# Attention with a feature map and an MLP mixer on one core: contracting the plain projections over 128 rows instead of 64

## The chip, the cores and the metric

The kernel runs on one core of one Trainium2 chip, in one launch. The metric is the device time of that core in microseconds, given as the median of three runs. A profiled execution has a time of its own and a span, which is the time from its first to its last instruction.

## The reference

For 8 batches of 8 heads, q, k and v have 576 tokens of 64 numbers. The feature map projects every token of q and k by the same 64 x 128 matrix, takes off the largest absolute value of the row, and joins exp(x) and exp(-x):

```python
def phi(x):
    proj = np.einsum('bhsd,df->bhsf', x, w_phi)
    proj = proj - np.max(np.abs(proj), axis=-1, keepdims=True)
    return np.concatenate([np.exp(proj), np.exp(-proj)], axis=-1)
```

From the mapped keys come kv (256 x 64 for each head) and z, their sum over tokens; the output of a head is phi(q) kv / (phi(q) z + 1e-6). The heads side by side give x, 576 x 512 for each batch. A token mixer follows, u = x + (relu(x^T W1) W2)^T with W1 576 x 256 and W2 256 x 576, and a channel mixer, u + relu(u C1) C2 with C1 512 x 1536 and C2 1536 x 512.

## The kernel before, in words

The 64 heads are worked on as 32 pairs. The first seven pairs (`PLAIN = 7`) are called plain: their attention matmuls are in float32, each of which TensorE runs as two passes. For a plain pair, `load_plain` (line 659) brings tiles named `pair` of 128 rows: rows 0 to 63 hold q, transposed, and rows 64 to 127 hold k. The other pairs take their rows split into a high and a low part (tiles `stk`, `stq`) against `wp2`.

`less_max` (line 611) makes the projection. For a plain pair it gets `base`, 64 for keys and 0 for queries, and contracts the 64 rows from there with the same 64 rows of `wp`, which holds the 64 x 128 matrix twice, one copy under the other. The output of one unit is 128 tokens x 128 features in a PSUM tile, named `ppk` for keys, `ppq` for queries and `ppt` for the odd 64 tokens of both queries of a pair. A plain pair has nine units of keys and nine of queries. VectorE then takes the largest absolute value (`mxk`, `mxq`, `mxt`, line 643) and subtracts it (`pmk`, `pmq`, `pmt`, line 645), and ScalarE makes the exponentials.

After that: `add_kv` (line 758) sums keys times values into `pkv`; `turn` (line 819) transposes the queries (`pt`); `numerators` (line 846) multiplies by kv (`pn`), and the denominators go through memory and back by small DMAs (`row`, `few`, `inv`, `den`). `token_mix` (line 899) has the tiles `px`, `pa`, `ph`; the channel mixer has `up_proj` (`h`) and `down_proj` (`acc`), lines 967 and 982. The mixer's weights come as 64-bit words, which `convert` (line 538) turns into high and low parts by one ScalarE, four VectorE, and again one ScalarE and one GpSimd instruction for each piece (tiles `bits`, `bitsc`).

Nothing is issued while this is written down. Five streams (keys, queries, tokens, weights, channels) record their instructions, and `arrange` (line 274) puts all of them in one order, by costs and due times that it works out itself: a plan of each engine's time, in which `cost` (line 198) gives each instruction a duration. For TensorE it holds a pass on part of the rows apart from a pass on all (lines 436 to 444): a part may run beside a part on other rows, and a change between parts and the whole costs 90 ns (`TURN`). It also keeps an own picture of TensorE's clock from an estimate of the work in it (`op.work`, line 215), in which a pass on 64 rows counts half. The order on TensorE prefers tokens, then keys and queries, then channels (lines 241 to 247). Setting up `wp` and `wp2` has lines 522 to 526; all recorded instructions show line 175 in the profile, so that they are told apart by their tiles.

Of the kernel before, what the change touches and what calls it, by code (L numbers as in the profile page):

```python
# [8 lines left out]
F32 = mybir.dt.float32  # L9
# [8 lines left out]
P = 128  # L18
B, H, S, D = 8, 8, 576, 64
NP = H // 2  # L20
F = 128
# [456 lines left out]
def mixer_kernel(ctx, tc, qk, qkp, vals, w_phi, w1, w1t, w2, wc1, wc2d, out):  # L478
    real, nc = tc.nc, Recorder()

    def pool(name, bufs, kind="sbuf", **kw):
        return Pool(ctx.enter_context(tc.tile_pool(name=name, bufs=bufs, **kw)), kind, bufs)

    cst = pool("cst", 1)
    wk = pool("wk", 2)
# [14 lines left out]
    def split(hi, lo, raw, eng_hi, eng_lo):  # L500

        if eng_hi is nc.scalar:
            nc.scalar.copy(hi, raw)
        else:
            eng_hi.tensor_copy(hi, raw)
        eng_lo.tensor_tensor(lo, raw, hi.bitcast(F32), op=ALU.subtract)
# [13 lines left out]
    eps = odd.tile([P, 1], F32, tag="eps", name="eps", bufs=1)  # L520
    nc.gpsimd.memset(eps, 1e-6)
    wp2 = st.tile([P, 2, F], F32R, tag="wp2", name="wp2", bufs=1)
    wp = cst.tile([P, F], F32, name="wp")
    nc.scalar.dma_start(wp[D:], w_phi)
    nc.scalar.dma_start(wp[:D], w_phi)
    split(wp2[:, 0], wp2[:, 1], wp, nc.vector, nc.vector)

    w1_h = cst.tile([P, 5, T], F32R, name="w1_h")
    w1_l = cst.tile([P, 5, T], F32R, name="w1_l")
# [81 lines left out]
    def less_max(ts, units, name, base=None):  # L611

        n, kind = len(units), name[0]
        if base == D and nplain["k"] < 5 * OPEN:
            ps = ps_a.tile([P, 2, 2, F], F32, tag=f"a{nplain['k'] % 2}", name=f"pp{name}")
        elif base == 0 and (nplain["q"] % 2 == 0 or nplain["q"] >= BORROWED):
            ps = ps_h.tile([P, 2, 2, F], F32, tag="h", name=f"pp{name}")
        elif kind == "k" or base == 0:  # L620
            ps = ps_w.tile([P, 2, 2, F], F32, tag="keys", name=f"pp{name}", bufs=1)
        else:
            ps = ps_w.tile([P, 2, 2, F], F32, name=f"pp{name}", **REST)
        if base is not None:
            nplain["k" if base else "q"] += 1
        for i, u in enumerate(units):
            t, c = (ts[1], 512) if u is None else (ts[u[0]], P * u[1])
            if base is None:
                nc.tensor.matmul(ps[:, i].rearrange("p two f -> p (two f)"), t[:, c:c + P],
                                 wp2.rearrange("p two f -> p (two f)"), start=True, stop=True)  # L630
            else:
                rows = slice(base, base + D)
                nc.tensor.matmul(ps[:, i, 0], t[rows, c:c + P], wp[rows], start=True, stop=True)
        if base is None:
            part = wk.tile([P, 2, F], F32, tag="part", name=f"part{name}")
            nc.scalar.copy(part[:, :n], ps[:, :n, 1])
            pr = wk.tile([P, 2, F], F32, tag="p", name=f"p{name}")
            nc.vector.tensor_tensor(pr[:, :n], ps[:, :n, 0], part[:, :n], op=ALU.add)
            pr, eng = pr[:, :n], nc.gpsimd
        else:  # L640
            pr, eng = ps[:, :n, 0], nc.vector
        mx = odd.tile([P, 2], F32, tag=f"mx{kind}", name=f"mx{name}")
        nc.vector.tensor_reduce(mx[:, :n], pr, axis=AX.X, op=ALU.max, apply_absolute_value=True)
        pm = wk.tile([P, 2, F], F32, tag=f"pm{kind}", name=f"pm{name}", bufs=1 if kind == "t" else 2)
        eng.tensor_tensor(pm[:, :n], pr, mx[:, :n].unsqueeze(2).to_broadcast([P, n, F]), op=ALU.subtract)
        return pm

# [20 lines left out]
    def keys():  # L668
# [3 lines left out]
        for i in range(B * NP):  # L672
# [9 lines left out]
            for g, us in enumerate(groups if i < PLAIN else blocks):  # L682
                pm = less_max(ts, us, f"k{i}_{g}", plain)
                if plain is None and g == 4:
                    kp = wk.tile([P, 1, 2, F], F32, tag="kt", name=f"kp{i}_{g}", bufs=1)
                elif plain is None and g % 2:
                    kp = wk.tile([P, 512], F32, tag="bits", name=f"kp{i}_{g}", bufs=3)
                    kp = kp.rearrange("p (n two f) -> p n two f", n=2, two=2)
                else:
                    kp = wk.tile([P, 2, 2, F], F32, tag="kp", name=f"kp{i}_{g}")  # L690
                for sg in range(2):
                    nc.scalar.activation(kp[:, :len(us), sg], pm[:, :len(us)], AF.Exp, scale=1.0 - 2.0 * sg)
                if plain is None:
                    sums(i, g, kp)
                yield 0.22
                for do, *args in todo:
                    do(*args)
                    yield 0.82
                if plain is not None:
                    todo = [(add_kv, i, g, us, kp, v_sb)]  # L700
                else:
                    todo = [(turn_kv, i, v_sb)] if g == 4 else []
# [82 lines left out]
    def queries():  # L785
# [3 lines left out]
        for piece in pieces:  # L789
            if split_up:  # L790
                yield from until(lambda: split_up[0] in kvs)
                numerators(*split_up)
                yield 0.75
            split_up = None
            if turned:
                split_up = turn(*turned)
                yield 0.25
            turned, made = made, None
            if piece:
                i, k, j = piece  # L800
                if (k, j) == (sides(i)[0], 0):
                    plain = 0 if i < PLAIN else None
                    if i < PLAIN:
                        yield from until(lambda: i in pairs)
                        ts = pairs[i]
                    else:
                        yield from until(lambda: i + 1 in raws or i + 1 == B * NP)
                        if i + 1 == B * NP:
                            load(i + 1)
                        ts = stack(raws[i + 1], 0, f"q{i}")  # L810
                    asked.add(i)
                if (k, j) == (0, 0):
                    tail = less_max(ts, [None], f"t{i}", plain)
                    yield 0.11
                pm = less_max(ts, [(j, 2 * k), (j, 2 * k + 1)], f"q{i}_{k}{j}", plain)
                made = (i, k, j, pm, tail)
                yield 0.22
# [312 lines left out]
```

## Time and profile before

| what | value |
|---|---|
| median of three runs | 1141.4 us (1139.65 to 1142.62) |
| profiled execution, its own time | 1142.8 us |
| span of that execution | 1141.0 us |
| PE busy | 1108.2 us, 97% of the span |
| PEld busy | 1033.7 us, 91% |
| DVE busy | 702.1 us, 62% |
| ACT busy | 629.2 us, 55% |
| POOL busy | 534.5 us, 47% |
| mean granted TensorE clock | 0.996 |

PE is TensorE's matmul stream, PEld its loads of stationary operands, which run beside it; DVE is VectorE, ACT ScalarE, POOL GpSimd, SP SyncE, which issues most DMAs. One pass is one load and one matmul. The ends of matmuls are modelled, so that the distance between the starts of two loads tells more of the pace than the busy time does.

### The profile page before, as it was taken

Reading aid. Unit: us, or ns where it says so; the run is one execution under the profiler, and the core shown is the slowest. Engines: PE = TensorE matmul, PEld = TensorE weight load, DVE = VectorE, ACT = ScalarE, POOL = GpSimd, SP = SyncE. Lnnn points to the kernel's source line nnn. Section 1 sums busy time; section 2 is a strip of 40 time slices with the busy share of each in tenths; the row PEclk is TensorE's granted clock in tenths of the full one; section 3 lists DMA queues with packets and bytes.
Section 4 is the critical chain, followed back from the end, with each engine's and each line's share of the span. In section 5 each row is a group of like instructions: output and inputs, shape, how many; then the busy total and the mean of one; then the engine's idle time right before and its main releaser. Section 6 shows DMA issues by size and latency. Waiting matters only on the chain.

```text
span 1141.0 us, 24085 instructions
## 1 busy us (share of the span) xinstructions
PE 1108.2 (97%) x8862; PEld 1033.7 (91%) x8862; DVE 702.1 (62%) x1558; ACT 629.2 (55%) x1749; POOL 534.5 (47%) x673
## 2 busy tenths in 40 slices
PE   8999999999999999999999999999999999999998
PEld 6788888788899989989999999999999999999998
DVE  4888875786667656767666666767676565211111
ACT  3887655666656566656666665665665555211110
POOL 1233426566556656456566556574664554011110
PEclk9999999998999999999999999999999999999999
DMA  6654521121121211211112111212121111000000
GB/s 180 170 155 133 138 83 46 50 61 40 44 51 45 63 44 45 59 45 48 39 48 59 39 52 44 63 45 58 49 59 24 46 28 31 12 20 20 20 20 20
DMA packets 60166, 65.42 MB, mean 57 GB/s; under 512 B 27344, under 2 KB 47056, under 8 KB 60048
## 3 DMA queue, kind: packets, MB, share of 16 engines
q1 hardware_dynamic: 59744, 63.48, 20.4%
q8 instruction: 70, 1.15, 0.4%
q14 instruction: 48, 0.39, 0.2%
q10 hardware_dynamic: 304, 0.40, 0.1%
HBM read 54.12 MB, written 9.73 MB: 56 GB/s over the span
## 4 chain that ended last, share of the span: by engine, by line
PE 80%; DMA 8%; DVE 5%; POOL 2%; ACT 2%; issue 2%; SPq 0%; ACTq 0%; DVEq 0%; POOLq 0%
PE acc L175 22%; PE h L175 22%; PE pkv L175 8%; PE pn L175 8%; PE pa L175 4%; PE ph L175 4%; PE ppk L175 4%; DMA den<-inv 4%; PE ppq L175 3%; PE pt L175 2%; DMA inv<-few 2%; PE px L175 2%; DMA few<-row 1%; DVE ks L175 1%; PE pkt L175 1%
## 5 line engine op out<-in xcount | busy, mean ns | idle before, releaser
L175 PE MATMUL acc<-gh,wc 128*128 128x256 f32 x1728 | 329.2, 280 | 1.1 <-ACT gh L175 0.9
L175 PEld LDWEIGHTS acc<-gh,wc 128*128 128x128 f32 x1728 | 272.5, 188 | 3.0 <-ACT gh L175 1.9
L175 PE MATMUL h<-uh,wc_h 128*128 128x256 f32 x864 | 242.9, 281 | 0.3 <-DVE gl L175 0.2
L175 PE MATMUL h<-uh,wc_l 128*128 128x256 f32 x864 | 242.3, 280 | 0.0
L175 PE MATMUL h<-ul,wc_h 128*128 128x256 f32 x864 | 242.0, 280 | 0.0
L175 PE MATMUL acc<-gl,wc 128*128 128x256 f32 x864 | 241.3, 280 | 0.0
L175 DVE SCALAR_TENSOR_TENSOR gl<-h,gh 128x512 fp32r<-128x512 f32 x108 | 74.5, 690 | 147.8 <-ACT gh L175 146.9
L175 PEld LDWEIGHTS h<-uh,wc_h 128*128 128x128 f32 x864 | 162.8, 188 | 2.8 <-issue 1.5
L175 PEld LDWEIGHTS h<-uh,wc_l 128*128 128x128 f32 x864 | 162.8, 188 | 0.8 <-issue 0.8
L175 PEld LDWEIGHTS acc<-gl,wc 128*128 128x128 f32 x864 | 162.6, 188 | 0.9 <-issue 0.8
L175 PEld LDWEIGHTS h<-ul,wc_h 128*128 128x128 f32 x864 | 162.6, 188 | 0.8 <-issue 0.8
L175 ACT ACTIVATE gh<-h 128x512 fp32r<-128x512 f32 x108 | 64.7, 599 | 138.0 <-PE h L175 137.3
L175 ACT ACTIVATE kp<-pmk 128x256 f32<-128x256 f32 (+1 forms) x320 | 107.7, 390 | 33.4 <-DVE pmk L175 12.7
L175 POOL TENSOR_TENSOR ql<-qf,qh 128x320 fp32r<-128x320 f32 (+1 forms) x100 | 83.8, 838 | 68.9 <-ACT qh L175 61.3
L175 POOL TENSOR_TENSOR ul<-xt,uh 128x64 fp32r<-128x64 f32 (+3 forms) x120 | 60.4, 533 | 113.9 <-ACT uh L175 113.1
L175 ACT COPY xt<-pn 64x256 f32<-64x256 f32 (+2 forms) x160 | 53.2, 345 | 108.3 <-DVE den L175 72.5
L175 ACT ACTIVATE qf<-pt 128x256 f32<-128x256 f32 (+1 forms) x256 | 103.3, 412 | 15.9 <-PE pt L175 14.3
L175 POOL TENSOR_TENSOR pmk<-pk,mxk 128x256 f32<-128x256 f32 (+1 forms) x125 | 79.7, 642 | 52.0 <-DVE mxk L175 33.0
L175 PE MATMUL pn<-qh,kv 128*128 128x320 f32 (+1 forms) x400 | 99.2, 300 | 2.9 <-DVE pt L175 1.4
L175 POOL TENSOR_TENSOR xt<-xt,den 128x256 f32<-128x256 f32 (+1 forms) x64 | 52.7, 823 | 93.4 <-DMA den<-inv 89.8
L175 POOL TENSOR_TENSOR pmq<-pq,mxq 128x256 f32<-128x256 f32 x100 | 63.6, 638 | 61.4 <-DVE mxq L175 49.7
L175 POOL TENSOR_TENSOR stq<-raw,stq 64x512 fp32r<-64x512 f32 (+1 forms) x50 | 74.1, 1481 | 36.3 <-ACT stq L175 32.5
(111 smaller groups left out, 2455.8 us busy)
## 6 DMA issues: line engine op xcount, KB each, us to landing
raw<-in_qk SPq DMA_DIRECT2D x24, 576.0 KB
rawc<-in_wc SPq DMA_DIRECT2D x24, 512.0 KB
v<-in_vals SPq DMA_DIRECT2D x31, 325.0 KB
den<-inv SPq DMA_DIRECT2D x64, 80.0 KB
den<-inv SPq DMA_DIRECT2D x64, 64.0 KB
out_x<-xt SPq DMA_DIRECT2D x12, 256.0 KB
out_x<-xt SPq DMA_DIRECT2D x16, 192.0 KB
pair<-in_qkp SPq DMA_DIRECT2D x7, 320.0 KB
```

The source lines that it names most:

```text
L175: return getattr(getattr(nc, self.unit), self.name)(*[real(a) for a in self.args], **{k: real(v) for k, v in self.kw.items()})
```

## The change

`wp` becomes two tables beside each other, each 128 rows high: table 0 has the matrix in rows 0 to 63 and zeros below, table 1 has zeros in rows 0 to 63 and the matrix below. A plain projection contracts all 128 rows of its `pair` tile with the table of its side. The split into `wp2` is made in two halves of 64 rows, and the tile `pmt` loses a half that was not used.

```diff
     wp2 = st.tile([P, 2, F], F32R, tag="wp2", name="wp2", bufs=1)
-    wp = cst.tile([P, F], F32, name="wp")
-    nc.scalar.dma_start(wp[D:], w_phi)
-    nc.scalar.dma_start(wp[:D], w_phi)
-    split(wp2[:, 0], wp2[:, 1], wp, nc.vector, nc.vector)
+    wp = cst.tile([P, 2, F], F32, name="wp")
+    for j in (1, 0):
+        rows = slice(j * D, j * D + D)
+        nc.gpsimd.memset(wp[rows, 1 - j], 0.0)
+        nc.scalar.dma_start(wp[rows, j], w_phi)
+    for j in range(2):
+        rows = slice(j * D, j * D + D)
+        split(wp2[rows, 0], wp2[rows, 1], wp[rows, j], nc.vector, nc.vector)
...
             else:
-                rows = slice(base, base + D)
-                nc.tensor.matmul(ps[:, i, 0], t[rows, c:c + P], wp[rows], start=True, stop=True)
+                nc.tensor.matmul(ps[:, i, 0], t[:, c:c + P], wp[:, base // D], start=True, stop=True)
...
-        pm = wk.tile([P, 2, F], F32, tag=f"pm{kind}", name=f"pm{name}", bufs=1 if kind == "t" else 2)
+        pm = wk.tile([P, 1 if kind == "t" else 2, F], F32, tag=f"pm{kind}", name=f"pm{name}",
+                     bufs=1 if kind == "t" else 2)
```

## Rows read from the trace of the kernel before

**Rows 1.** Busy time by stretch: us, PE, PEld, DVE, ACT, POOL, clock, DMA, GB/s.
```profile
9.00:28.40 19.40, 19.40 (x78) 16.39 (x78) 11.85 (x31) 8.38 (x23) 3.04 (x2) 1.00 0.59 157
28.40:60.00 31.60, 29.25 (x209) 24.67 (x208) 27.20 (x74) 27.02 (x76) 7.26 (x8) 1.00 0.56 158
60.00:116.00 56.00, 55.66 (x361) 46.05 (x359) 47.78 (x110) 42.98 (x114) 18.84 (x17) 1.00 0.58 147
116.00:185.00 69.00, 65.58 (x485) 59.19 (x485) 52.30 (x95) 40.62 (x95) 29.63 (x30) 1.00 0.31 93
...
240.00:285.00 45.00, 40.58 (x283) 34.97 (x283) 32.07 (x75) 28.27 (x83) 26.01 (x33) 0.89 0.17 47
285.00:965.00 680.00, 667.82 (x5532) 631.50 (x5531) 453.31 (x1025) 414.44 (x1189) 395.20 (x503) 1.00 0.18 47
965.00:1141.00 176.00, 171.51 (x1500) 171.07 (x1498) 35.20 (x65) 29.56 (x71) 17.34 (x30) 1.00 0.07 20
...
80.00:100.00 20.00, 19.88 (x130) 16.72 (x129) 17.82 (x41) 15.26 (x40) 8.36 (x8) 1.00 0.41 105
```

**Rows 2.** The plain projections' loads, by tile: count, duration ns min/median/max, first and last start.
```profile
L175 PEld LDWEIGHTS ppk<-wp,pair x126: 182/188/335, 3.7 to 116.1; 64*128 64x128 f32 x126
L175 PEld LDWEIGHTS ppq<-wp,pair x112: 182/188/334, 6.4 to 183.0; 64*128 64x128 f32 x112
L175 PEld LDWEIGHTS ppt<-wp,pair x14: 183/186/330, 7.2 to 156.5; 64*128 64x128 f32 x14
```

**Rows 3.** Timeline of PEld, 90 us: start, duration, merged instructions.
```profile
90.17 0.24 PEld L175 LDWEIGHTS pt<-ident,pmq 128*128 128x128 f32 x2
90.58 0.52 PEld L175 LDWEIGHTS ppq<-wp,pair 64*128 64x128 f32 x4 [0.17 <-PE ph L175]
91.22 0.74 PEld L175 LDWEIGHTS pkv<-v,kp 128*128 128x128 f32 x6
```

**Rows 4.** Timeline of PEld, 9 to 13 us.
```profile
9.03 1.78 PEld L175 LDWEIGHTS pkv<-v,kp 128*128 128x128 f32 x8 [0.22 <-issue]
10.99 1.78 PEld L175 LDWEIGHTS ppq<-wp,pair 64*128 64x128 f32 x8 [0.18 <-issue]
13.00 0.29 PEld L175 LDWEIGHTS pt<-ident,pmq 128*128 128x128 f32 x2 [0.22 <-issue]
```

**Rows 5.** Timeline of PEld: runs of 64-row loads, the first, one on the way, the last.
```profile
30.25 0.29 PEld L175 LDWEIGHTS ppt<-wp,pair 64*128 64x128 f32 x2
...
115.98 0.29 PEld L175 LDWEIGHTS ppk<-wp,pair 64*128 64x128 f32 x2
...
182.67 0.52 PEld L175 LDWEIGHTS ppq<-wp,pair 64*128 64x128 f32 x4 [0.43 <-DVE gl L175]
```

**Rows 6.** Timeline of PE: keys and queries side by side, the first, and three at full pace.
```profile
6.36 0.58 PE L175 MATMUL ppq<-wp,pair 64*128 64x128 f32 x1 [1.40 <-DMA wp<-in_w_phi]
...
35.51 0.27 PE L175 MATMUL ppq<-wp,pair 64*128 64x128 f32 x1
35.52 0.27 PE L175 MATMUL ppk<-wp,pair 64*128 64x128 f32 x1
35.62 0.27 PE L175 MATMUL ppq<-wp,pair 64*128 64x128 f32 x1
```

**Rows 7.** Timeline of PE, 24 to 31 us.
```profile
24.62 1.06 PE L175 MATMUL ppk<-wp,pair 64*128 64x128 f32 x4
25.61 2.50 PE L175 MATMUL pn<-qf,kv 128*128 128x320 f32 x4
...
28.40 1.93 PE L175 MATMUL pkv<-v,kp 128*128 128x104 f32 x16
```

**Rows 8.** Timeline of DVE, from 6 us.
```profile
6.42 0.23 DVE L175 CAST wp<-wp 128x128 fp32r<-128x128 f32 x1 [6.42 <-DMA wp<-in_w_phi]
6.68 0.29 DVE L175 TENSOR_TENSOR wp<-wp,wp 128x128 fp32r<-128x128 f32 x1
```

## The prediction

> **What bounds the kernel now.** I read the table of engines first and then the busy time by stretch, because the share over the whole span hides three different stages. After 285 us PE is busy 667.82 of 680 us, and the last 176 us hold almost nothing but the mixer's matmuls, with VectorE at 35.20 [rows 1]. That last stretch is work which TensorE couldn't place earlier. So TensorE's time saved anywhere comes off the end, as long as the instant at which it was saved has something else for TensorE to do. The plain projections all lie before 185 us [rows 2], and there VectorE is near its limit too: 27.20 of 31.6 us, 47.78 of 56, and at its densest 17.82 of 20, a share of 0.89 [rows 1]. Before 28.4 us it has room, 11.85 of 19.4, and PE is busy without a gap.
>
> Busy time hides what matters here, so I then went through the timeline of PEld. There are 126 + 112 + 14 = 252 passes on 64 rows [rows 2], in runs between passes on 128 rows. At 90 us the four loads of such a run last 0.52 us, the last one 0.19, so loads start every (0.52 - 0.19)/3 = 0.11 us. Two loads of pt at 90.17 should let the run begin at 90.39; it begins at 90.58, 0.19 late. Its four loads should let pkv begin at 91.02; it begins at 91.22, 0.20 late [rows 3]. Going to 64 rows and back costs **0.39 us a run**, though PE counts as busy. Transposes, pkv and pn follow each other without such a gap.
>
> Early passes are slower. Between 9 and 13 us eight loads last 1.78 us, (1.78 - 0.33)/7 = 0.21 us each, and the two turns of that run cost 1.96 - 8 x 0.21 = 0.28 and 2.01 - 8 x 0.21 = 0.33 [rows 2, 4]. At 28.40 us sixteen passes of pkv take 1.93 us; eight had taken 1.78 us in loads alone at 9.03 [rows 4, 7]. [...] Up to 24.62 us runs of 64-row passes come between the others all the time; the first stretch without any, pn from 25.61 on, is the one behind which the pace doubles [rows 7].
>
> **The change part by part.** *Turns removed.* The timeline has 39 runs of 64-row passes between 30.25 and 182.67 us: 9 up to 60, 23 up to the one at 115.98, 7 behind it [rows 5]. At 0.39 us that is 3.5, 9.0 and 2.7 us. Between 9 and 28.4 us there are five, at 0.6 us: 3.0 us.
>
> *Overlap lost.* Where a key run and a query run meet, they share the array: at 35.51 and 35.52 one pass of each starts, the next at 35.62, so two passes go in the time of one [rows 6]. I count 32 such pairs from 6.36 us on: 8 at the slow pace, 18 up to 60, 6 later. Contracted over all rows they follow one another: 8 x 0.21 = 1.7, 18 x 0.11 = 2.0, 6 x 0.11 = 0.7 us lost. [...]
>
> *One pass itself.* A 128-row float32 pass with a 128-wide operand isn't in this part of the trace; the nearest, pkv with 104 columns, runs at 0.11 us as the projections do [rows 3, 7], and I take no difference.
>
> *The clock.* The rows bound this by nothing (the pace rises at 28.4 as before) and by a rise as soon as TensorE is filled from 9 us on. I take the second end, nearer to the only rise there is: it came 2.8 us after pn had followed the last 64-row run [rows 7], and the changed kernel has none. With some us for a later start I put it at 13 us. Of the 15.4 us up to 28.4, 2.4 are turns counted above; 13.0 us of slow passes become 6.5.
>
> *What of this VectorE lets through.* In each stretch I take the smaller of TensorE's saving and the time that VectorE would have left at its densest share, 0.89 [rows 1]. From 9 to 28.4: TensorE 3.0 - 1.7 + 6.5 = 7.8, VectorE 19.4 - 11.85/0.89 = 6.1; so 6.1. Up to 60: 3.5 - 2.0 = 1.5 against 31.6 - 27.20/0.89 = 1.0; so 1.0. Up to 116: 9.0 - 0.7 = 8.3 against 56 - 47.78/0.89 = 2.3; so 2.3. Up to 185: 2.7 against 69 - 52.30/0.89 = 10.2; so 2.7. What isn't let through turns into waits of PE for VectorE. The sum is **12.1 us**. If the weights' conversion, which is the movable part of VectorE's work, is put elsewhere by the new order, up to 1.3 + 1.5 + 8.3 + 2.7 + 6.5 = 20.3 us.
>
> *The rest.* Two memsets go to POOL, which is busy 3.04 of 19.4 us just after; they run while the DMAs of the matrix land and cost nothing. The split on VectorE takes four instructions for two, 0.23 + 0.29 = 0.52 us more if half the rows take as long [rows 8], and the first reduction queues behind it; the key half, which lands first, may also leave earlier. I take 0, with ends of -2.7 (the first projections start at 3.7, and the split holds VectorE's queue until 6.42 [rows 2, 8]) and +0.5. `pmt` costs nothing: the same elements are written. The two DMAs stay on ACT's queue in their order. The `pair` and weight loads on SP and the denominators' round trips move with the buffers that they wait for; I find no one queued behind them that isn't also freed sooner. The whole order is worked out anew, since durations and clock in the plan change. That has no row; the nearest is the disturbed stretch from 240 to 285 us, where PE is busy for 40.58 of 45 us and the clock is 0.89: (1 - 0.89) x 45 = 5.0 us [rows 1]. One such stretch may go or come; I take none and keep 5 us either way.
>
> The profiled execution took 1142.8 us: 1142.8 - 12.1 = 1130.7. It stood 1.4 us above the median, so I forecast **1129 us** for the median.
>
> **The rivals.** *All of it arrives.* The new order shifts conversions and VectorE doesn't bind: 1142.8 - 20.3 - 1.4 = 1121 us. For it: VectorE is busy only 52.30 of 69 us behind 116. Against: the weights must be there before the channel mixer can fill TensorE's time.
>
> *The clock rises when it did.* Then the first stretch gives 1.3 and the sum is 7.3: 1134 us. For it: one rise is a thin base, and the rows can't part the missing 64-row runs from other differences. [...]
>
> *Nothing arrives.* VectorE and the denominators' round trips set the pace up to 185 us, and PE's saved time becomes waits: 1141 us. For it: VectorE's 85% between 28 and 116. Against: PE waits there for hardly anything, 55.66 of 56 us busy. That the edit doesn't do what it says would show the same: no run of passes closing up.
>
> *Slower: TensorE outruns VectorE and the clock falls.* Place: 28 to 285 us. Gaps on PE like those between 240 and 285 us take the clock down, and each such stretch costs 5.0 us. Two more of them (10.0) against the low saving of 7.3 leave +2.7, no change; the third decides, 15.0 - 7.3 = +7.7: 1149 us. For it: 6 us of TensorE's saving between 60 and 116 can't pass VectorE. Against: between 28 and 60 VectorE's share is as high, PE has 2.35 us of gaps, and the clock column stays at 1.00 [rows 1].
>
> **How the numbers follow.** The forecast has 0.50, all of it 0.12, the clock unmoved 0.15, nothing 0.13, slower 0.10. A difference of 0.3% (3.4 us) is about what a measurement of this kernel can tell from none. So faster 0.77, within it 0.13, slower 0.10. The range goes from 1119, below the second case, to 1141, which takes in the forecast with 5 us either way, the unmoved clock and part of the fourth; the slower case and some of the ends stay out.
>
> **What would show it.** The loads of ppk, ppq and ppt in the form 128*128, 252 of them, 0.11 us apart with no 0.2 us before and behind. The pace of pkv near 0.11 us from about 13 us on; at 28 us, as before, my clock step is wrong. The run of ppk that stands at 115.98 some 9 us earlier. New waits of PE for mxk, pmk or qf between 30 and 116 us are what VectorE kept back; if they sum to 10 us, nothing arrives. Behind 285 us the passes should be the same and shifted by the gain; a loss there, or a clock under 1.00 in more places than 240 to 285, makes the prediction wrong.

## The result and the profile after

The changed kernel takes **1126.0 us** (median of 4 runs, 1125.26 to 1126.45); the kernel before, run again beside it, takes 1140.6 us. The ratio is 0.987, with a 95% interval of 0.985 to 0.989: 14.6 us faster, where 12.1 were forecast. The profiled execution has a span of 1124.1 us and a time of 1126.0 us. That of the kernel before stood 2.2 us above the new median, so spans alone overstate the gain (16.9 us), and so do the distances that are read from the two traces below.

The busy time by stretch of the changed kernel, with the columns of [rows 1]:

```profile
9.00:28.40 19.40, 18.78 (x143) 17.69 (x142) 16.47 (x45) 13.10 (x36) 1.27 (x1) 1.00 0.47 139
28.40:60.00 31.60, 28.38 (x203) 24.92 (x201) 24.64 (x67) 24.90 (x73) 6.66 (x8) 1.00 0.63 164
60.00:116.00 56.00, 52.66 (x383) 47.28 (x384) 46.06 (x105) 45.86 (x122) 19.11 (x18) 1.00 0.52 147
116.00:185.00 69.00, 59.48 (x451) 54.35 (x451) 61.36 (x106) 39.92 (x89) 38.68 (x36) 1.00 0.33 101
...
240.00:285.00 45.00, 43.38 (x355) 40.85 (x354) 33.19 (x75) 29.13 (x82) 28.60 (x36) 1.00 0.25 64
285.00:965.00 680.00, 672.14 (x5569) 636.60 (x5568) 447.19 (x1021) 414.07 (x1189) 395.36 (x501) 1.00 0.18 46
```

Three things differ from [rows 1]. Between 9 and 28.4 us TensorE gets through 142 loads instead of 78, and VectorE does 16.47 us of work instead of 11.85. Between 28.4 and 185 us PE has more gaps: 3.2 + 3.3 + 9.5 = 16.1 us against 6.1 us before; behind 116 VectorE is at 61.36 of 69, a share of 0.89. And from 240 to 285 us the clock stays at 1.00 (before: 0.89), with 1.6 us of gaps on PE instead of 4.4.

The loads of the keys' projections by tile (as [rows 2]) and the timeline of PEld (as [rows 3, 4]):

```profile
L175 PEld LDWEIGHTS ppk<-wp,pair x126: 186/192/338, 6.3 to 111.0; 128*128 128x128 f32 x126
```

```profile
6.33 1.78 PEld L175 LDWEIGHTS ppk<-wp,pair 128*128 128x128 f32 x8 [6.33 <-issue]
...
10.41 2.45 PEld L175 LDWEIGHTS pkv<-v,kp 128*128 128x128 f32 x14
12.79 0.75 PEld L175 LDWEIGHTS ppq<-wp,pair 128*128 128x128 f32 x6
13.45 0.25 PEld L175 LDWEIGHTS pt<-ident,pmq 128*128 128x128 f32 x2
...
14.01 0.30 PEld L175 LDWEIGHTS pkv<-v,kp 128*128 128x128 f32 x2
14.23 0.53 PEld L175 LDWEIGHTS ppk<-wp,pair 128*128 128x128 f32 x4
14.68 0.97 PEld L175 LDWEIGHTS pkv<-v,kp 128*128 128x128 f32 x8
```

From pkv at 14.01 to ppk at 14.23 two loads take 0.22 us, from ppk to pkv at 14.68 four take 0.45: no turn is left. The eight passes from 6.33 still come 0.21 us apart; the six from 12.79 come 0.11 apart. From 10.41 to 12.79 there are 14: if 0.21 us holds for the first n and 0.11 for the rest, 2.38 = 0.11 x 14 + 0.10 n gives n = 8, so the pace doubles at about 12.2 us instead of 28.4. The packed trace lists TensorE's granted clock as stretches, each with a start and a level, 1.0 or 0.5 in both of these kernels. The first stretch at the full level, 1.0, begins at 12.1 us in the changed kernel and at 28.2 us in the kernel before.

The tile kf holds the sums of a split pair (one that isn't plain). When it is first written, and when last, tells how far a kernel has come. Tile view of the kernel before, the changed one, and x_all below:

```profile
L175 DVE COPY kf<-pkv x25: 650/692/693, 204.6 to 934.8; 128x512 f32<-128x512 f32 x25
```

```profile
L175 DVE COPY kf<-pkv x25: 650/692/694, 197.3 to 918.0; 128x512 f32<-128x512 f32 x25
```

```profile
L179 DVE COPY kf<-pkv x25: 650/692/693, 192.5 to 922.1; 128x512 f32<-128x512 f32 x25
```

At the first kf the changed kernel is only 7.3 us ahead, at the last 16.8. So more than half of the gain came where the edit changes no instruction. This had to be settled: what is worth the rows, and what the new order?

### The profile page after: what moved, and what is told of

It is laid out like the page before. It is cut to its first block, busy times and chain, and to the rows that moved or that the text cites. A ratio compares the mean times of both kernels' runs of the same rounds, so it can differ in the third digit from the quotient of the medians.

```text
span 1124.1 us, 24086 instructions
## 1 busy us (share of the span) xinstructions
PE 1087.0 (97%) x8862; PEld 1024.3 (91%) x8862; DVE 702.0 (62%) x1560; ACT 629.2 (56%) x1749; POOL 540.4 (48%) x675
## 4 chain that ended last, share of the span: by engine, by line
PE 75%; DMA 10%; DVE 6%; POOL 3%; ACT 3%; issue 2%; SPq 1%; POOLq 0%; ACTq 0%; DVEq 0%
PE acc L175 22%; PE h L175 21%; PE pn L175 7%; PE pkv L175 7%; PE pa L175 4%; DMA den<-inv 4%; PE ppk L175 3%; PE ph L175 3%; DMA inv<-few 3%; PE ppq L175 2%; PE pt L175 2%; DVE bitsc L175 2%; DMA few<-row 2%; PE px L175 1%; DMA row<-den 1%
## 5 line engine op out<-in xcount | busy, mean ns | idle before, releaser
L175 ACT ACTIVATE kp<-pmk 128x256 f32<-128x256 f32 (+1 forms) x320 | 108.2, 390 | 28.2 <-DVE pmk L175 11.6
L175 ACT ACTIVATE qf<-pt 128x256 f32<-128x256 f32 (+1 forms) x256 | 103.4, 412 | 15.5 <-PE pt L175 13.8
```

What stands on the lines that cost most here:

```text
L175: return getattr(getattr(nc, self.unit), self.name)(*[real(a) for a in self.args], **{k: real(v) for k, v in self.kw.items()})
```

## The experiments

**Rows and order taken apart.** In x_all every instruction keeps its place in the order of the kernel before, and only what a projection contracts is exchanged while it is issued (the split takes four instructions, two memsets come first). y_half is the reverse.

```diff
 # x_all, on the kernel before; wz is the padded table
                 nc.tensor.matmul(ps[:, i, 0], t[rows, c:c + P], wp[rows], start=True, stop=True)
+                r = slice(0, P) if True else rows
+                nc.ops[-1].alt = lambda to, o=ps[:, i, 0], x=t[r, c:c + P], y=wz[r, base // D]: to.tensor.matmul(
+                    o.made(), x.made(), y.made(), start=True, stop=True)
 # y_half, on the changed kernel
                 nc.tensor.matmul(ps[:, i, 0], t[:, c:c + P], wp[:, base // D], start=True, stop=True)
+                r = slice(base, base + D)
+                nc.ops[-1].alt = lambda to, o=ps[:, i, 0], x=t[r, c:c + P], y=wp[r, base // D]: to.tensor.matmul(
+                    o.made(), x.made(), y.made(), start=True, stop=True)
```

> All plain projections over 128 rows with padded weights, but every instruction in the order of the kernel before (only two memsets ahead and the split into four are added). Theory A (the passes themselves: turns gone, clock up early, VectorE letting part of it through): it gains most of what the changed kernel gained, 10 to 14 us, so 1127 to 1131 us; pkv passes 0.11 us apart from about 13 us on. Theory B (the new order does it, by where the clock falls and where PE waits behind 200 us): it gains 7 us or less, 1134 us or more, and the stretch near 240 to 285 us with a clock under 1.00 is still there.

> The changed kernel's order of every instruction, but each plain projection contracts its own 64 rows. Theory A: the turns are back (0.4 to 0.6 us for some 44 runs) and the clock is low until some 28 us, while this order puts fewer key and query runs side by side: 1138 to 1146 us. Theory B: the order keeps most of the gain, 1133 us or less.

| | 64 rows | 128 rows |
|---|---|---|
| order of the kernel before | 1140.5 us | x_all 1129.85 us, ratio 0.990 (0.988 to 0.992) |
| order of the changed kernel | y_half 1143.2 us, ratio 1.002 (1.000 to 1.004) | 1126.0 us, ratio 0.987 (0.985 to 0.989) |

Theory A holds. The rows alone, in an unchanged order, give 10.7 us. The new order alone gives nothing: it is 2.7 us slower, at the edge of its interval. Together they give 14.6, but the intervals of that ratio and x_all's overlap a little, so that the 3.9 us between them are likely rather than shown. x_all is 12.1 us ahead at the first kf and 12.7 at the last: it gains all of it by 205 us and keeps it. One sign of Theory B is there too, the clock's fall near 240 us. Its waits of PE from 235 to 255 us and its row by stretch:

```profile
PE pn L179 <- DVE pt L179: 1.4, 1, 1.4
PE ppq L179 <- DVE den L179: 1.1, 1, 1.1
PE ppq L179 <- ACT qh L179: 0.9, 1, 0.9
```

```profile
240.00:285.00 45.00, 40.26 (x291) 36.22 (x292) 30.15 (x67) 27.44 (x77) 27.61 (x34) 0.92 0.16 45
```

Here PE has 4.7 us of gaps and the clock 0.92, that is (1 - 0.92) x 45 = 3.6 us; the changed kernel has 1.6 us and 1.00. The fall goes with the order: all seven traces in the old order (the kernel before, x_all and five of the runs below) have one that begins between 238 and 256 us; of the four in the new order only w_after, below, has one near there, at 261 us.

That doesn't make the fall the source of the gain. The last 7,023 of TensorE's 8,862 passes name the same tiles in the same sequence in all four kernels, so that the time can be split there:

| kernel | this sequence begins at | and lasts to the end |
|---|---|---|
| before (old order, 64 rows) | 285.57 us | 855.4 us |
| x_all (old order, 128 rows) | 272.67 us | 855.6 us |
| y_half (new order, 64 rows) | 291.45 us | 851.2 us |
| changed (new order, 128 rows) | 273.15 us | 851.0 us |

The rows are worth 12.9 us in the old order and 18.3 in the new, all of it before the sequence begins. The new order loses 5.9 us (64 rows) or 0.5 us (128 rows) up to there, although it has no fall, and gains 4.2 or 4.6 us behind. So the changed kernel, 4.8 us behind x_all at the first kf, has made that up by 273 us, about where x_all has its fall, and all that it is ahead in the end comes from the same passes behind. The first 2,000 of them, in x_all and then in the changed kernel, and two waits of x_all there:

```profile
272.67:522.30 249.63, 243.69 (x2002) 228.73 (x2001) 167.70 (x379) 153.24 (x445) 148.17 (x191) 1.00 0.19 48
```

```profile
273.15:519.00 245.85, 242.56 (x2003) 228.53 (x2001) 166.07 (x379) 154.26 (x447) 150.61 (x192) 1.00 0.18 48
```

```profile
PE pn L179 <- DVE pq L179: 1.2, 1, 1.2
PE pn L179 <- POOL ql L179: 0.6, 1, 0.6
```

The clock is full in both. PE's gaps are 5.9 us in x_all and 3.3 in the changed kernel, which has only 0.3 us of these two waits. What in the new order shortens them no run takes apart. In the seven traces in the old order the sequence lasts 853.3 to 855.6 us (the 853.3 is l_before's, below, with less work for VectorE and a fall of the clock in it); in the three in the new order that have no fall of the clock in it, 851.0 to 851.2.

**Clock and turns taken apart.** As x_all, with 128 rows for some pairs only:

```diff
-                r = slice(0, P) if True else rows
+                r = slice(0, P) if pair < 2 else rows
 # in x_late: pair >= 2
```

> Order of the kernel before; only the pairs 0 and 1 contract 128 rows, the pairs 2 to 6 their 64. Clock theory (64-row runs held the clock down): pkv passes at 0.11 us from 11 to 15 us on instead of 28, and a gain of 5 to 7 us, 1134 to 1136 us. Rival (the rise has nothing to do with rows): the pace doubles at about 28 us as before, and only five slow turns are saved less eight overlaps, about 1.3 us: 1139 us.

> Order of the kernel before; pairs 0 and 1 contract 64 rows, the pairs 2 to 6 128. The clock should rise at about 28 us as before. Turn theory: 39 turns of 0.39 us less 24 overlaps of 0.11 us, 12.6 us, of which VectorE lets 6 to 9 through: 1132 to 1135 us. Rival (VectorE and the round trips set the pace between 28 and 185 us): within 2 us of the kernel before, 1139 to 1141 us, with as much new waiting on PE.

x_early takes 1134.5 us (ratio 0.995, 0.993 to 0.997), 6.1 us less. x_late takes 1136.7 us (0.997, 0.996 to 0.999), 3.8 us less, between its two theories, so that neither range held. Their sum, 9.9, is close to x_all's 10.7. The pkv loads on the timeline of PEld, x_early and then x_late:

```profile
9.44 1.29 PEld L179 LDWEIGHTS pkv<-v,kp 128*128 128x128 f32 x8
...
12.72 0.97 PEld L179 LDWEIGHTS pkv<-v,kp 128*128 128x128 f32 x8
```

```profile
20.29 1.78 PEld L179 LDWEIGHTS pkv<-v,kp 128*128 128x128 f32 x8 [0.22 <-issue]
...
28.86 2.11 PEld L179 LDWEIGHTS pkv<-v,kp 128*128 128x128 f32 x16
```

Eight loads take 0.97 us from 12.72 on in x_early, and still 1.78 us at 20.29 in x_late, whose pace rises at about 29 us. The first stretch at the full level is listed from 10.1 us in x_early and from 29.4 us in x_late. Same order, same inputs: with the 64-row runs of the pairs 0 and 1 passes came (1.78 - 0.33)/7 = 0.21 us apart and the full level began 19.3 us later, so these runs held the clock down. Whether it is the half-filled array or the turns, which come with every such run, x_early and x_late don't tell.

**What kept the rest back.** TensorE's side promised more than 10.7 us. Two of the four VectorE instructions of each converted weight piece are left out in both kernels here:

```diff
 # l_before on the kernel before, l_xall on x_all; the same line behind the shift
         nc.vector.tensor_scalar(m.bitcast(F32), m.bitcast(F32), LEAST, MOST, op0=ALU.max, op1=ALU.min)
+        nc.ops[-1].alt = lambda to: None
```

> The kernel before without two of the four VectorE instructions of each converted piece of the mixer's weights (the clamp and the shift are left out, some 0.42 us each, 27 us of VectorE in all up to 176 us). If VectorE sets the pace of the first 185 us here: 5 to 15 us off, 1126 to 1135 us. If TensorE does: within 3 us of the kernel before.

> x_all (order of the kernel before, all plain projections over 128 rows) with the same two VectorE instructions left out. Theory (VectorE let only part of TensorE's saving through, 11 to 12 of about 20 us): the distance to l_before grows from 10.7 us to 14 to 20 us. Rival (what was kept back waits for something else, ScalarE or the denominators' round trips): the distance stays at 9 to 12 us.

l_before takes 1140.7 us (ratio 1.001, 1.000 to 1.003): 27 us less of VectorE buy nothing, as expected if TensorE sets the pace with 64 rows. l_xall takes 1125.7 us (0.988, 0.986 to 0.990). The distance grows from 10.7 to 15.0 us, into the theory's range. That VectorE had kept back these 4 us is likely, not shown: the intervals of x_all and l_xall overlap, and the traced clock rose at 14.0 us in x_all but at 9.9 in l_xall, and 4.1 us less at half pace (0.21 us a pass instead of 0.11) are worth about 2.0 us. VectorE can also be relieved with nothing left out. Here the clamp moves to GpSimd, with a new order:

```diff
-        nc.vector.tensor_scalar(m.bitcast(F32), m.bitcast(F32), LEAST, MOST, op0=ALU.max, op1=ALU.min)
+        nc.gpsimd.tensor_scalar(m.bitcast(F32), m.bitcast(F32), LEAST, MOST, op0=ALU.max, op1=ALU.min)
```

> The changed kernel with the clamp of the weights' conversion on GpSimd instead of VectorE, and the order worked out anew. VectorE has 13 us less up to 176 us, GpSimd about 40 us more, of which it has room for in every stretch (38.68 of 69 us busy from 116 to 185). If VectorE keeps back part of the gain and nothing takes its place: 1 to 4 us off, 1122 to 1125 us. Rival (the slower clamp lengthens the chain of each piece and VectorE waits in it, or the new order brings clock falls): 1126 to 1132 us.

It takes 1150.6 us (ratio 1.010, 1.008 to 1.012), worse than even the rival's range. Waits up to 200 us, and the stretch where the clock falls:

```profile
POOL bitsc L175 <- ACT bitsc L175: 16.2, 9, 4.6
DVE bitsc L175 <- POOL bitsc L175: 13.8, 13, 3.1
```

```profile
240.00:285.00 45.00, 37.94 (x259) 34.30 (x258) 27.76 (x59) 22.73 (x69) 25.34 (x34) 0.87 0.17 43
```

VectorE waits 13.8 us in its own queue for the slower clamp, more than the 13 us of work that it was spared (GpSimd is busy for 108.7 us from 9 to 185 us, 65.7 in the changed kernel), and PE's gaps from 240 to 285 us grow to 7.1 us with a clock of 0.87. The clock also falls at 113 and 171 us; all its falls together last 20.4 us at a level of 0.5 and cost about 10 of the 24.6 us by which this kernel is behind the changed one. Since the order is new too, the slower clamp isn't shown to be the whole cause.

**The start.** In the changed kernel the first projection comes at 6.33 us, not at 3.7 [rows 2]: the plan had put the values' load ahead of the matrix on ACT's queue. f_after puts the matrix first, but there its tile exists before the plan is made, and, against what was expected of it, the whole order changes; f2_after leaves the order alone.

```diff
 # f2_after, on the changed kernel
         nc.scalar.dma_start(wp[rows, j], w_phi)
+        nc.ops[-1].alt = lambda to: None
...
     with tc.manual_schedule():
+        for j in (1, 0):
+            real.scalar.dma_start(wp[j * D:j * D + D, j].made(), w_phi)
```

> The changed kernel with the two loads of the matrix issued ahead of the values' load on the ACT queue; all else in its order. The first projection should start at about 3.8 us, as in the kernel before, instead of 6.4. If the late start is carried to the end: up to 2.5 us off, 1123.5 to 1125 us. Rival (the pair tile or the splits on VectorE hold the first reduction anyway): no difference.

> The changed kernel with the two loads of the matrix issued ahead of the values' load on the ACT queue, this time with the order of all other instructions word for word that of the changed kernel. First projection at about 3.8 us instead of 6.4. If the late start is what the changed order gives away up to 200 us (it gained 7.3 us there, x_all 12.1): up to 2.5 us off, 1123.5 to 1125 us, and the sums of pair 7 (the first kf) 2 to 2.5 us earlier. Rival (the first reduction is held by something else, or the gain turns into waits): within 1 us of 1126.

f_after takes 1126.9 us (0.990, 0.988 to 0.992), which says little since its order differs. f2_after takes 1125.95 us (0.988, 0.987 to 0.990): no difference to the changed kernel. Its timeline, and of its waits of PE up to 60 us the longest for VectorE and the one for the values:

```profile
3.83 1.78 PEld L179 LDWEIGHTS ppk<-wp,pair 128*128 128x128 f32 x8 [3.83 <-issue]
...
6.15 0.22 DVE L179 CAST wp<-wp 64x128 fp32r<-64x128 f32 x1 [0.64 <-DMA wp<-in_w_phi]
...
10.20 3.06 PEld L179 LDWEIGHTS pkv<-v,kp 128*128 128x128 f32 x14 [1.45 <-ACT kp L179]
```

```profile
PE ppq L179 <- DVE pmq L179: 1.6, 2, 1.1
...
PE pkv L179 <- DMA v<-in_vals: 1.2, 1, 1.2
```

The first pkv starts at 10.20 us, only 0.2 us earlier than in the changed kernel, and the first kf at 197.6 us, 0.3 later. The 2.5 us won at the start are spent on waits, among them VectorE's for the second half of the matrix and one for the values that now come later; the rival holds.

**The clock raised ahead.** TensorE multiplies the identity by itself while it waits for the first data:

```diff
 # w_before on the kernel before, w_after on the changed one; fw_after is f_after with 8
     with tc.manual_schedule():
+        heat = ps_k.pool.tile([P, 2, 2, P], F32, tag="kv", name="heat")
+        for _ in range(12):
+            real.tensor.matmul(heat[:, 0, 0], ident.made(), ident.made(), start=True, stop=True)
```

> The kernel before, with 12 float32 matmuls of the identity by itself (24 passes over 128 rows) on TensorE ahead of its first projection, while it waits for data; 64-row projections and the order are as before. Clock theory (64-row runs keep a low clock low, but a high one up, as behind 28 us): pkv passes 0.11 us apart from 9 us on and a gain like that of x_early, 5 to 8 us: 1133 to 1136 us. Rival (64-row runs also take a high clock down again early on): pkv back at 0.21 us somewhere between 10 and 28 us, gain under 3 us.

> The changed kernel with the same 12 matmuls ahead. Its first 29 or so passes, up to 12.2 us, ran 0.21 us apart; at 0.11 us TensorE has 2.8 us less to do there. If TensorE sets the pace at the start: 1 to 3 us off, 1123 to 1125 us. Rival (the chain through VectorE and ScalarE sets it from the first reduction on): no difference, 1126 us.

> Both: the matrix loaded first and 8 matmuls of the identity ahead. If both starts matter and add: 3 to 5 us off, 1121 to 1123 us. If VectorE takes over as the bound at the start, no more than the better of the two alone.

w_before takes 1135.2 us (0.996, 0.993 to 0.998), 5.1 us less, with every projection on 64 rows. The time is that of the clock theory, but part of the rival is there too (timeline of PEld, then the row by stretch):

```profile
17.42 0.52 PEld L175 LDWEIGHTS pkv<-v,kp 128*128 128x128 f32 x4 [0.51 <-ACT kp L175]
...
20.00 0.93 PEld L175 LDWEIGHTS ppk<-wp,pair 64*128 64x128 f32 x4 [1.41 <-issue]
```

```profile
20.00:30.00 10.00, 9.97 (x48) 8.29 (x49) 7.08 (x21) 6.31 (x17) 2.25 (x3) 0.67 0.39 117
```

The high clock fell again at 20 us, behind 64-row runs and a gap of 1.41 us (four loads take 0.93 us at 20.00), and came back before 30 (loads start 0.11 us apart at 27.68). x_early, in the same order but with 128 rows at this place, has a gap there too, of 1.16 us, and keeps the full pace, four loads in 0.52 us:

```profile
20.42 0.52 PEld L657 LDWEIGHTS ppk<-wp,pair 128*128 128x128 f32 x4 [1.16 <-PE ppq L657]
```

So padding likely does more than raise the clock early: it keeps the clock up too. The two gaps differ by 0.25 us, and no run parts gap and rows.

w_after was a miss: 1130.7 us (0.992, 0.991 to 0.994), 4.6 us slower than the changed kernel, though its order is the same and it is ahead at the first kf. The rows by stretch show where it lost:

```profile
260.00:270.00 10.00, 9.59 (x64) 8.12 (x65) 6.98 (x18) 5.78 (x18) 4.82 (x8) 0.83 0.12 28
380.00:390.00 10.00, 9.88 (x65) 9.71 (x65) 6.93 (x17) 4.80 (x15) 6.53 (x9) 0.83 0.07 15
```

Two falls of the clock cost 2 x (1 - 0.83) x 10 = 3.4 of the 4.6 us. fw_after takes 1131.2 us (0.991, 0.988 to 0.995) with six runs from 1122.4 to 1133.9, and shows falls at 150, 170 and 240 to 260 us, with a mean clock of 0.994; it decides nothing. No variant beat the changed kernel clearly.

## Why the prediction was right, point by point

The range held the time and the forecast was 3 us off. That the gain of 14.6 us lies so near the 12.1 is partly luck: one term was about 2 us too large, and another, taken as 0, was worth about 4. The parts came out as follows.

*Turns and overlap.* Right in kind: 128-row passes follow each other 0.11 us apart with nothing in front or behind. Mis-sized: of the 6.0 us that VectorE was to let through behind 28.4 us, x_late shows 3.8, with an interval of 1.4 to 5.1. The last load of ppk, wanted some 9 us earlier than at 116, is at 106.6 us in x_all, but at 111.0 in the changed kernel's order. Two readings in the sum were slightly off, without weight, because VectorE's limit was the smaller term in both stretches: 24 runs, not 23, lie from 60 to 116 us, and four of the eight slow pairs lie ahead of 9 us. The two changes of a run cost 0.39 us [rows 3], and a pair of passes side by side saves 0.11 us [rows 6]. Here the changes outweigh the pairs: x_late removes both behind 28.4 us, and is 3.8 us faster.

*The clock.* Right in kind and size: 12.2 us against my 13 (the list of stretches has the full level from 12.1 us, and from 28.2 in the kernel before), and 6.1 us in x_early where the first stretch's term was 6.1. That doesn't show VectorE's limit in this stretch: x_early's trace is 7.9 us ahead at the first kf (196.7 us), as much as TensorE's own saving of 7.8.

*What VectorE lets through.* l_xall speaks for the cap without showing it. But I took the new order to be the old one with less in it, or a better one. It moved conversions behind 116 us: their tile bitsc takes 44.6 us of VectorE there instead of 36.2, VectorE as a whole went from 52.30 to 61.36 of 69 us, and PE's gaps from 3.4 to 9.5. At the first kf only 7.3 us had arrived, where x_all, in the old order, had 12.1. My test for failure, new waits of PE for mxk, pmk or qf that sum to 10 us between 30 and 116 us, wasn't met. All such waits, in the kernel before and in the changed one:

```profile
PE ppk L175 <- DVE pmk L175: 1.7, 2, 0.8
PE pn L175 <- ACT qf L175: 0.5, 1, 0.5
```

```profile
PE ppk L175 <- DVE pmk L175: 2.6, 3, 1.4
```

That is 0.4 us more, where by my sum 6.5 us (0.5 up to 60, 6.0 up to 116) were kept back. PE's gaps of all kinds grew by 3.9 us from 28.4 to 116 us, and by 6.1 behind.

*The rest.* "The two DMAs stay on ACT's queue in their order" left something out: the values' load went ahead of both, and the first pass came 2.6 us later. It cost nothing, as f2_after shows. "Behind 285 us the passes should be the same and shifted by the gain" was half right: they are the same, in the same sequence, but the shift grows from 12.4 us where this sequence begins to 16.9 at the end.

*The stretch from 240 to 285 us.* I kept 5 us either way for it and took none. The fall went, and with it 5.0 us of clock, but that was no net gain: x_all, which has the fall, is still 0.5 us ahead of the changed kernel where the common sequence begins. So the second term that was mis-sized is the effect of the new order: I took 0, and it was about 4 us of 14.6, a loss until 200 us that is made good by 273 us, and a gain behind, in passes that stayed the same.

## What to carry to other kernels

Half the rows can cost more than all of them: where short runs on part of TensorE's array stand between full ones, count what each change costs (0.39 us a run here) and how many runs really meet a partner (0.11 us a pair here) before giving the rows away. Where an order is worked out from costs, an edit's own effect is told only by running it in the old order, and the old form in the new one; the rows were worth 10.7 us here in the one and 17.2 in the other. Time won at one place came back here as a wait (f2_after, 1.2 us for the values alone) or with falls of the clock far behind it (w_after, 3.4 us), so small improvements should be read from the whole trace. Where two orders end in the same sequence of passes, the instant at which it begins tells at once on which side of it a gain was made.

## What was not expected of the hardware

The clock column reads 1.00 up to 28 us in [rows 1] while passes come at half pace, 0.21 us apart and not 0.11, and 0.67 from 20 to 30 us in w_before once the clock had been up: before the first rise in these traces the column doesn't show the level, the distance between loads does. The list of stretches has nothing there (it begins at 28.2 us), and the column counts that as full. And a kernel with the same order on every engine was 4.6 us slower with 24 passes more at its start: w_after's two falls, at 261 and 380 us, lie far from its only edit, and why they come there isn't shown.
